# Cos-MLP in three steps an output, weight preparation on an agenda, gate logits from float16 blocks

## The chip, the cores and the metric

One core of a Trainium2 chip runs the whole program. The metric is device time in microseconds, the median of several executions. One further execution was recorded by the hardware profiler; what is said of single instructions comes from that one. Engines carry the names of the profile: PE is TensorE (PEld its weight loads), DVE is VectorE, ACT is ScalarE, POOL is GpSimd, and SP is the queue from which every DMA of this kernel is issued.

## The reference

Three layers follow each other on 2304 tokens of width 512 (4 batches of 576 positions, 8 heads of 64).

```
x = attention(q, k, v, f)                   # causal, with a decay from the running sum of log f
h = x @ w_in;  x = (h * cos(h)) @ w_out     # 512 -> 2048 -> 512; w_in and w_out are float64
logits = x @ w_gate                         # 8 experts
P = exp(logits - max);  8 times: rows to 1, columns to N / 8
out = sum over e of P[:, e] * (relu(x @ w1[e]) @ w2[e])     # 512 -> 1024 -> 512
```

The middle layer is called the Cos-MLP here.

## The kernel before, in words

**Numbers.** A large matmul is made of float16 products. Each operand is scaled by a power of two and split into a high and a low half; three products (high·high, high·low, low·high) give one result. The scale comes from a sum of squares a partition (ScalarE, `Square` with an accumulated output), whose maximum over all partitions everyone needs. `share` (L117) reduces on VectorE, stores the maxima to a small DRAM tensor and at once issues the DMA that reads them back to every partition; `set_scale` (L124) reduces what came back and makes the scale with six small operations on VectorE.

**The queues.** The order of the work is written out by hand (`tc.manual_schedule`): each engine runs its instructions in the order in which the program issues them, and an instruction that waits holds all that are behind it on its engine. SP's DMAs are in order in the same way. Side work (weights, surveys, splits) is written as Python generators; each `next` issues one more piece of them between the pieces of the main work.

**Attention** runs up to about 273 us. Between its steps the generators prepare the first two pairs of Cos-MLP weights (`prepare_pair`, L195) and split the first group of tokens.

**Cos-MLP** (L1227 to L1275). Three groups of 768 tokens, four blocks `b` of hidden units with two pairs of tiles each: 24 items `(b, g, s)`. An item computes four outputs `o` of 128 hidden units by 384 tokens. TensorE gets the first layer of the item (4 × 12 matmuls, L270), then the second layer of the item two before (4 × 12 matmuls, L921). Four PSUM banks hold the first layer's outputs. For every output, all within one turn of the loop: ScalarE takes the whole turns of the phase (L298), VectorE the rest (L299), ScalarE the Sin (L303), VectorE the product (L307, after which the bank is free); one turn later ScalarE casts the high half (L312) and POOL, or VectorE in the last block, subtracts the low half (L314). `leave2` adds a second-layer result to `acc` (ScalarE in block 0, L935; VectorE later, L937).

In between, `later` (L1183) prepares a pair of weight tiles for each three items or so. Four jobs of one 512 KB load each turn float64 bits into float32: POOL L177, VectorE L178, L180, L182 and L185, ScalarE L186. Then come one share of two columns into `room`, the scale, ScalarE's scaling and cast (L212, L214) and POOL's low halves (L218). `load_job` issues the load after next. `split_group` (L236) scales a token group and splits it on ScalarE and POOL, and `find_group` finds its scale. `survey_first` reads expert 0's weights in 16 chunks to find their scale.

At the end the scales of groups 0 and 1 for the experts are found (`look_x`, `share_x`, `set_x`), and the gate logits of these groups are taken as float32 matmuls of `acc` and `w_gate` (`logits`, L939). `expert_prep` makes the first expert's weights and the seven blocks of group 0's input.

**Experts** (from L1593). Sixteen blocks (expert, half) of three token groups each; a group's turn is two first layers (L1370) and one second layer (L1491). `hook` is called 28 times a group, 84 times a block, and issues what `put_at` planned for that slot: weights of the next block, a survey of the next expert's weights (`plan_survey`, L1568), its scale, and in the first two blocks the other groups' inputs, the logits of group 2 and the Sinkhorn steps.

Of the kernel before, what the change touches and what calls it, by code (L numbers as in the profile page):

```python
# [23 lines left out]
def kernel(  # L24
# [13 lines left out]
    nc = tc.nc  # L38
# [39 lines left out]
    sel = const.tile([16, 8], F32, name="sel")  # L78
# [18 lines left out]
    most = keep.tile([P, 2], F32, name="most")  # L97
    sc_w = [keep.tile([P, 2], F32, name=f"scw{x}") for x in range(NW)]
    bk_w = [keep.tile([P, 2], F32, name=f"bkw{x}") for x in range(NW)]
# [5 lines left out]
    xsum = [keep.tile([P, KD], F32, name=f"xsum{x}") for x in range(2 * NG)]  # L105
    sc_x = [keep.tile([P, 1], F32, name=f"scx{x}") for x in range(2 * NG)]
    bk_x = [keep.tile([P, 1], F32, name=f"bkx{x}") for x in range(2 * NG)]
# [16 lines left out]
    def set_scale(room_, k, scale, back):  # L124
        nc.vector.tensor_reduce(back, room_.rearrange("q (p x) -> q x p", x=k), axis=AX.X, op=ALU.max)
# [19 lines left out]
    def share_x(y):  # L145
        share(xsum[y], 1, f"xmost{y}", xroom_of[y])

    def set_x(y):
        set_scale(xroom_of[y], 1, sc_x[y], bk_x[y])


# [18 lines left out]
    def run_job(n):  # L170
# [6 lines left out]
        nc.gpsimd.tensor_tensor(guard, topf, topf, ALU.mult)  # L177
        nc.vector.tensor_scalar(xi, top, 3, 0x3FFFFFFF, ALU.logical_shift_left, ALU.bitwise_and)  # L178
        yield
        nc.vector.scalar_tensor_tensor(xi, top, -0x40000000, xi, ALU.bitwise_and, ALU.bitwise_or)  # L180
        yield
        nc.vector.scalar_tensor_tensor(xi, low, 29, xi, ALU.logical_shift_right, ALU.bitwise_or)  # L182
        load_job(n + 2)
        yield
        nc.vector.scalar_tensor_tensor(x, guard, TINY * TINY, x, ALU.is_ge, ALU.mult)  # L185
        nc.scalar.activation(guard, x, AF.Square, accum_out=wsum[:, y // 2, y % 2 : y % 2 + 1])  # L186
        yield
# [7 lines left out]
    def prepare_pair(u, early):  # L195
        for y in range(4):
            yield from run_job(4 * u + y)
        share(wsum, 2, f"wmost{u}", room)
        yield
        yield  # L200
        yield
        set_scale(room, 2, sc_w[u], bk_w[u])
        nc.vector.tensor_tensor(both[:, u : u + 1], bk_w[u][:, 0:1], bk_w[u][:, 1:2], ALU.mult)
        yield
        todo = [(tmps[y], d(u, 0), d(u, 1), sc_w[u][:, y : y + 1]) for y, d in enumerate((in_of, out_of))]
        for t, hi, lo, sc in todo:
            if early:
                nc.gpsimd.tensor_scalar(t, t, sc, 0.0, ALU.mult, ALU.add)
                yield
                nc.gpsimd.tensor_scalar(hi, t, 1.0, 0.0, ALU.mult, ALU.add)  # L210
            else:
                nc.scalar.activation(t, t, AF.Copy, scale=sc)  # L212
                yield
                nc.scalar.copy(hi, t)  # L214
            yield
        for t, hi, lo, sc in todo:
            for c in range(0, 2 * DM, 2 * P):
                nc.gpsimd.tensor_tensor(lo[:, c : c + 2 * P], t[:, c : c + 2 * P], hi[:, c : c + 2 * P], ALU.subtract)  # L218
                if c % DM:
                    yield  # L220
# [3 lines left out]
    def find_group(g, junk):  # L224
        for x in range(KD):
            look_x(g, g, junk, x)
            if x % 2:
                yield
        share_x(g)
        yield  # L230
        yield
        yield
# [3 lines left out]
    def split_group(g):  # L236
        X = X_of[g]
        for x in range(KD):
            a = acc[:, x, group(g)]
            nc.scalar.activation(a, a, AF.Copy, scale=sc_x[g])  # L240
            yield
            for t in range(2):
                a = acc[:, x, cols(g, t)]
                hi, lo = (X[PLACE[x // 2, t]][:, y, x % 2, :] for y in range(2))
                nc.scalar.copy(hi, a)
# [4 lines left out]
    xroom_of = [xroom] * (NG + 1) + [None, None]  # L250
# [44 lines left out]
    def phase(b, g, s, o, ps):  # L295
        t = draw("t")
        sc = turnv[:, 2 * b + s, g : g + 1]
        nc.scalar.activation(t.bitcast(I32), ps, AF.Identity, bias=quarter, scale=sc)  # L298
        nc.vector.scalar_tensor_tensor(t, ps, sc, t.bitcast(I32), ALU.mult, ALU.subtract)  # L299
        return t  # L300
# [9 lines left out]
    def split_h(b, g, s, o, G):  # L310
        H = draw(f"t{o % 2}")
        nc.scalar.copy(H[:, 0, :], G)  # L312
        eng = nc.vector if b == NW // 2 - 1 else nc.gpsimd
        eng.tensor_tensor(H[:, 1, :], G, H[:, 0, :], ALU.subtract)  # L314
        H_of[b, g, s, o] = H

    with tc.manual_schedule():

        with ExitStack() as actx:
# [141 lines left out]
            nc.gpsimd.tensor_tensor(sel, ident[0:16, 0:8], ident[0:16, 8:16], ALU.add)  # L461
# [321 lines left out]
            pieces = chain(prepare_pair(0, True), prepare_pair(1, True))  # L783
# [37 lines left out]
            for x in range(-9, NSTEP + PS):  # L821
# [7 lines left out]
                if x == 8 * PS + 6:  # L829
                    splitting = chain(find_group(0, junk), split_group(0))  # L830
                if x == 12 * PS + 6:
                    splitting = chain(splitting, find_group(1, junk))
                if x >= 4 and x % 2 == 0:
# [809 lines left out]
```

## Time and profile before

| | |
|---|---|
| median of 3 runs | 2123.81 us (2122.56 to 2125.36) |
| the profiled execution | 2126.4 us, its span 2124.6 us |
| TensorE | busy 1979.3 us, 93% of the span |
| VectorE | 1471.5 us, 69% |
| ScalarE | 1269.9 us, 60% |
| GpSimd | 1110.6 us, 52% |
| mean granted TensorE clock | 0.975 |

The span runs from the first to the last instruction. A busy share is a mean over stages of different kinds. In a row of groups, the time behind the bar is the sum of the group's instructions, then the mean of one, then how long the engine stood idle just before them, and what ended that idle time.

### The profile page before, as it was taken

What the parts mean: (1) busy time and instruction counts of PE and PEld (TensorE: products, weight loads), DVE (VectorE), ACT (ScalarE), POOL (GpSimd) and SP (SyncE); (2) the same over time, 40 slices, a digit from 0 to 9 for tenths busy, and PEclk for the clock granted to TensorE, in tenths of its full rate; (3) what the DMA queues carried; (4) which work ended last, traced back from release to release, by engine and by line L of the source; (5) the groups of instructions that cost most, each with busy time, mean ns of one, the idle gap of its engine ahead of it and who ended that gap; (6) DMA issues with size and microseconds to landing.
All of it is one profiled execution on the core that took longest, in us unless ns stands there. A gap on an engine that the chain in (4) does not pass through costs nothing.

```text
span 2124.6 us, 41207 instructions
## 1 busy us (share of the span) xinstructions
PE 1979.3 (93%) x15493; PEld 1446.6 (68%) x15493; DVE 1471.5 (69%) x3385; ACT 1269.9 (60%) x2698; POOL 1110.6 (52%) x1439
## 2 busy tenths in 40 slices
PE   7897859788999998999999999999999999999998
PEld 6786735454556666677777777677777767777776
DVE  8878745566655345778777777777777777777776
ACT  6787756564556457656556656556656655655543
POOL 7676634333434357655465555554555645555531
PEclk9999989999999899999999999999999999999999
DMA  5444311232010013313303203313223222321122
GB/s 133 101 97 103 51 32 52 67 97 48 21 33 11 24 63 122 115 46 127 95 31 126 102 21 132 100 35 120 63 85 107 75 81 69 107 85 45 49 83 60
DMA packets 145128, 160.19 MB, mean 75 GB/s; under 512 B 68128, under 2 KB 96928, under 8 KB 144928
## 3 DMA queue, kind: packets, MB, share of 16 engines
q1 hardware_dynamic: 144928, 157.55, 25.5%
q8 instruction: 122, 2.00, 0.4%
q14 instruction: 78, 0.64, 0.1%
HBM read 142.20 MB, written 10.39 MB: 72 GB/s over the span
## 4 chain that ended last, share of the span: by engine, by line
PE 64%; DVE 7%; DMA 7%; ACT 5%; POOL 2%; issue 2%; SPq 0%; DVEq 0%; POOLq 0%; ACTq 0%
PE y L1491 17%; PE y L1370 15%; PE bq L1491 13%; PE bq L1370 11%; PE a L921 4%; PE ph L270 3%; DMA xs<-emost 2%; DMA room<-wmost 1%; DMA emost<-most 1%; DVE tm L185 1%; DMA wmost<-most 1%; DVE tm L180 1%; DVE t L307 1%; DMA xmost<-most 1%; DVE t L299 1%
## 5 line engine op out<-in xcount | busy, mean ns | idle before, releaser
L1491 PEld LDWEIGHTS <-h 128*128 128x128 f16 x6048 | 595.3, 98 | 77.6 <-DVE h L1396 0.5
L1370 PEld LDWEIGHTS <-wi 128*128 128x128 f16 x4032 | 395.5, 98 | 289.3 <-issue 37.4
L1370 PE MATMUL y<-xc,wi 128*128 128x384 f16 x2304 | 431.5, 327 | 27.6 <-DVE bq L1390 18.0
L1405 POOL TENSOR_TENSOR h<-t,h 128x384 f16<-128x384 f32 x192 | 175.3, 913 | 480.5 <-ACT h L1404 460.3
L1491 PE MATMUL y<-wb,h 128*128 128x256 f16 x3456 | 415.0, 275 | 0.0
L1370 PE MATMUL bq<-xc,wi 128*128 128x384 f16 x1728 | 329.7, 327 | 0.8 <-ACT t L1386 0.8
L1386 ACT ACTIVATE t<-y 128x384 f32<-128x384 f32 x192 | 94.2, 491 | 377.9 <-PE y L1370 377.9
L1491 PE MATMUL bq<-wb,h 128*128 128x256 f16 x2592 | 307.1, 273 | 0.2 <-DVE h L1396 0.2
L270 PE MATMUL ph<-xc,wi 128*128 128x384 f16 x1152 | 211.4, 344 | 54.8 <-DVE t L307 54.8
L1472 DVE SCALAR_TENSOR_TENSOR acc<-y,gate,acc 128x256 f32<-128x256 f32 x504 | 212.5, 477 | 50.8 <-PE y L1491 50.2
L270 PEld LDWEIGHTS <-wi 128*128 128x128 f16 x1152 | 117.8, 102 | 144.2 <-issue 78.3
L921 PE MATMUL a<-h,wo 128*128 128x384 f16 x1152 | 197.4, 332 | 11.6 <-DVE acc L937 11.2
L1472 DVE SCALAR_TENSOR_TENSOR acc<-bq,gate,acc 128x256 f32<-128x256 f32 x378 | 159.6, 478 | 40.0 <-PE bq L1491 39.6
L921 PEld LDWEIGHTS <-wo 128*128 128x128 f16 x1152 | 114.4, 99 | 90.5 <-issue 18.4
L1396 DVE TENSOR_TENSOR h<-bq,h 128x384 f16<-128x384 f32 x288 | 157.3, 550 | 8.5 <-ACT h L1393 6.5
L314 POOL TENSOR_TENSOR h<-t,h 128x384 f16<-128x384 f32 x72 | 66.7, 927 | 183.2 <-ACT h L312 164.1
L1390 DVE SCALAR_TENSOR_TENSOR bq<-bq,t 128x384 f32<-128x384 f32 x192 | 107.6, 561 | 70.5 <-PE bq L1370 65.6
L1393 ACT CAST h<-bq 128x384 f16<-128x384 f32 x288 | 136.0, 486 | 12.5 <-DVE bq L1447 12.3
L1390 DVE SCALAR_TENSOR_TENSOR bq<-y,t 128x384 f32<-128x384 f32 x96 | 54.3, 565 | 119.9 <-PE y L1370 102.9
L1399 POOL TENSOR_TENSOR h<-st,h 128x384 f16<-128x384 f32 x96 | 88.0, 916 | 83.8 <-ACT h L1393 82.8
L1403 ACT ACTIVATE t<-bq 128x384 f32<-128x384 f32 x192 | 94.7, 493 | 37.5 <-DVE bq L1390 35.6
L299 DVE SCALAR_TENSOR_TENSOR t<-ph,turnv,t 128x384 f32<-128x384 f32 x96 | 58.8, 613 | 64.2 <-ACT t L298 64.1
(250 smaller groups left out, 3360.4 us busy)
## 6 DMA issues: line engine op xcount, KB each, us to landing
xc<-xd SPq DMA_DIRECT2D x105, 384.0 KB
xs<-in_moe_w_dram SPq DMA_DIRECT2D x112, 256.0 KB
sg<-in_moe_w_dram SPq DMA_DIRECT2D x44, 512.0 KB
wo<-in_moe_w_dram SPq DMA_DIRECT2D x20, 512.0 KB
sg<-in_moe_w_in_dram SPq DMA_DIRECT2D x16, 512.0 KB
sg<-in_moe_w_out_dram SPq DMA_DIRECT2D x16, 512.0 KB
xd<-xc SPq DMA_DIRECT2D x14, 384.0 KB
q<-q SPq DMA_DIRECT2D x30, 160.0 KB
```

Of the source, the lines that this page charges most:

```text
L270: nc.tensor.matmul(ps[:, 0:HN], w[ws][:, (2 * kk + f) * P : (2 * kk + f + 1) * P], X_of[g][PLACE[kk // 2, t]][:, xs, kk % 2, :], start=n == 0,
L921: nc.tensor.matmul(ps[:, 0:HN], out_of(2 * b + x, ws)[:, f * DM + d * P : f * DM + (d + 1) * P], H[:, hs, :], start=n == 0, stop=n == 11,)
L1370: nc.tensor.matmul(ps[:, 0:HN], w[:, ws, a, k, :], X[b][:, xs, k, :], start=fresh and n == 0, stop=n == 5, skip_group_check=not fresh,)
L1386: nc.scalar.activation(c, cut(ps), AF.Copy, scale=RAISE)
L1390: nc.vector.scalar_tensor_tensor(cut(c), cut(ps), RAISE, other, ALU.mult, ALU.add)
L1393: nc.scalar.copy(HT[m][c][:, 0, :], src)
L1396: nc.vector.tensor_tensor(HT[m][c][:, 1, :], src, HT[m][c][:, 0, :], ALU.subtract)
L1399: nc.gpsimd.tensor_tensor(HT[m][c][:, 1, :], src, HT[m][c][:, 0, :], ALU.subtract)
L1403: nc.scalar.activation(r, cut(ps), AF.Relu)
L1405: nc.gpsimd.tensor_tensor(HT[m][c][:, 1, :], r, HT[m][c][:, 0, :], ALU.subtract)
L1472: nc.vector.scalar_tensor_tensor(a, v, gate[:, tt, e : e + 1], a, ALU.mult, ALU.add)
L1491: nc.tensor.matmul(ps[:, at_ * HD : (at_ + 1) * HD], HT[m][a][:, s1, c * P : (c + 1) * P], W2T[side][m][:, s2, b, :], start=fresh and m == ...
```

## The change

It touches the Cos-MLP, the scales and the first two expert blocks.

- **Outputs in steps.** `phase` becomes `whole` and `rest`, `split_h` becomes `high_h` and `low_h`. A new `step` issues, in this order: whole turns of output o, product of o−2, Sin of o−1, rest of o, low half of o−3, a piece of weight work, high half of o−2. Three empty steps follow the last output. The second layer is issued in the step of the item's second output, and one `leave2` in each step. In item (0, 0) the low halves go to VectorE.
- **Agenda.** `plan_pair` writes each operation of a pair into a numbered step. A pair's jobs are 5 steps apart (4 in the attention), the second pair starts 30 (21) steps after the first; share, fetch and set lie 6 (2) steps apart, and each column has its own share. Two agenda steps an output are issued in items 0 and 1, four in items 2 to 5, three later; what is left is issued when a block of items ends.
- **Scales.** `share` no longer issues the fetch; `fetch` is a call of its own. All shares have one column. `find_x` finds two of the groups' scales by a transpose and a matmul on TensorE in place of the DMAs.
- **Logits.** `w_gate` is scaled and split into float16 halves early (`split_gate`). The logits of all three groups are taken in the experts' first block, in slots 16, 40 and 54, from the float16 blocks of the experts' input: 60 matmuls a group with 16 columns. VectorE puts the two halves together in three operations. The Sinkhorn steps start in slot 58.
- **Split of groups.** Group 1's high halves are copied on POOL; group 2's split begins at the end of item 2.
- **Surveys.** Experts 0 and 1 are both surveyed within the Cos-MLP. The later ones start with expert 2 in the third block; looks lie at slots 8, 10 and then every third from 38, each chunk's load one slot after the look that frees its buffer; share, fetch and set in slots −5, 1 and 11 around the block's end.

```diff
-    def share(cols, k, name, room_):
-        m = most[:, 0:k]
-        d = sdram.tile([P, k], F32, name=name)
+    def share(cols, name):
+        m = mosts[n % len(mosts)]
+        shared[name] = sdram.tile([P, 1], F32, name=name)
         nc.vector.tensor_reduce(m, cols, axis=AX.X, op=ALU.max)
-        nc.sync.dma_start(d, m)
-        nc.sync.dma_start(room_, d.rearrange("p x -> (p x)").partition_broadcast(P))
+        nc.sync.dma_start(shared[name], m)
+
+    def fetch(name, room_):
+        nc.sync.dma_start(room_, shared[name].rearrange("p x -> (p x)").partition_broadcast(P))
...
+    def find_x(y, bank):
+        gm, gr = mosts[y % 3], mosts[3 + y % 3]
+        nc.vector.tensor_reduce(gm, xsum[y], axis=AX.X, op=ALU.max)
+        yield
+        ps = bank()
+        nc.tensor.transpose(ps[0:1, 0:P], gm, ident)
+        nc.vector.tensor_reduce(gr[0:1, 0:1], ps[0:1, 0:P], axis=AX.X, op=ALU.max)
+        yield
+        ps = bank()
+        nc.tensor.matmul(ps[:, 0:1], ones[0:1, :], gr[0:1, 0:1], start=True, stop=True)
+        nc.vector.tensor_copy(bk_x[y], ps[:, 0:1])
+        make_scale(sc_x[y], bk_x[y])
+        yield
...
+    def plan_pair(agenda, u, base, gap, lag, early):
+        for y in range(4):
+            plan_job(4 * u + y, lambda n, fn, y=y: at_(gap * y + n, fn), gap)
+        for y, d in enumerate((in_of, out_of)):
+            n = gap * (2 * y + 1) + 7
+            at_(n, lambda y=y: share(wsum[:, y, :], f"wmost{u}{y}"))
+            at_(n + lag, lambda y=y, row=row: fetch(f"wmost{u}{y}", row))
+            n += 2 * lag
+            at_(n, lambda row=row, sc=sc, bk=bk: set_scale(row, sc, bk))
...
+        def logits(g, X, bank):
+            for x in range(TT):
+                t, c = divmod(x, TT // 2)
+                todo = [(B11, 0), (B21, 2)] if t == 0 else [(T1, 0), (B11, 0), (B22, 2)]
+                for blk_, k0 in todo:
+                    for k in range(2):
+                        for y in range(2):
+                            nc.tensor.matmul(
+                                ps[:, x * 2 * NE : (x + 1) * 2 * NE],
+                                X[blk_][:, y, k, c * P : (c + 1) * P],
+                                wg[:, k0 + k].rearrange("p y e -> p (y e)"),
...
+        def step(new):
+            if new:
+                key, ps = new
+                t = whole(*key, ps)
+            m = None
+            if waved:
+                mk, mps, mt = waved.pop(0)
+                m = (*mk, product_of(*mk, mps, mt))
+            if shaped:
+                z = shaped.pop(0)
+                wave(z[2])
+                waved.append(z)
+            if new:
+                rest(*key, ps, t)
+                shaped.append((key, ps, t))
+            if high_:
+                low_h(*high_.pop(0))
+            next(pieces, None)
+            if m:
+                high_h(*m)
+                high_.append(m)
...
             for o in range(4):
+                step(((b, g, x, o), outs[o]))
+                if n >= 2 and o == 1:
+                    pb, pg, _ = items[n - 2]
+                    rest_of = layer2(pb, pg, x)
+                if waiting:
+                    leave2(*waiting.pop(0))
+                waiting += rest_of
+                next(pieces, None)
+                next(looking, None)
+                next(splitting, None)
...
-            first, step = (53, 2) if blk == 0 else (2, 5)
             for n in range(NSEEN):
-                put_at(base + first + step * n, lambda n=n: (look(e, n), load_chunk(e, n + 2)))
+                when = (8, 10)[n] if n < 2 else 32 + 3 * n
+                put_at(base + when, lambda n=n: look(e, n))
+                put_at(base + (when + 1 if n >= 2 else 16 + 2 * n), lambda n=n: load_chunk(e, n + 2))
```

## Rows read from the trace of the kernel before

**Rows 1.** Stretches (start:end, length, busy us of each engine, granted clock, DMA, GB/s).

```profile
391.60:547.40 155.80, 130.63 (x770) 75.98 (x769) 98.29 (x191) 82.66 (x171) 56.84 (x64) 0.98 0.26 72
547.40:679.70 132.30, 127.29 (x770) 75.86 (x769) 78.49 (x152) 73.05 (x125) 56.82 (x74) 0.97 0.10 26
...
751.30:837.10 85.80, 77.32 (x529) 55.42 (x528) 43.05 (x107) 59.76 (x138) 62.48 (x73) 0.92 0.17 58
```

**Rows 2.** Timeline of TensorE (start, length, line, output, count, idle time before).

```profile
299.21 7.00 PE L270 MATMUL ph<-xc,wi 128*128 128x384 f16 x24 [5.34 <-DVE t L307]
...
547.39 7.96 PE L270 MATMUL ph<-xc,wi 128*128 128x384 f16 x48
555.19 7.96 PE L921 MATMUL a<-h,wo 128*128 128x384 f16 x48
...
695.29 7.99 PE L944 MATMUL ph<-wgr,acc 128*128 128x8 f32 x48
703.13 6.43 PE L270 MATMUL ph<-xc,wi 128*128 128x384 f16 x24
...
734.92 6.79 PE L944 MATMUL ph<-wgr,acc 128*128 128x8 f32 x48
741.55 9.90 PE L921 MATMUL a<-h,wo 128*128 128x384 f16 x48
751.30 1.14 PE L1370 MATMUL y<-xc,wi 128*128 128x384 f16 x6
```

**Rows 3.** Groups of instructions, 264 to 752 us (count, busy us, mean ns, idle before).

```profile
L270 PE MATMUL ph<-xc,wi 128*128 128x384 f16 x1152 | 211.4, 344 | 54.8 <-DVE t L307 54.8
...
L298 ACT ACTIVATE t<-ph,quarter,turnv 128x384 int32<-128x384 f32 x96 | 63.3, 659 | 57.7 <-PE ph L270 32.2 <-DVE turnv L289 21.7 <-DVE down L291 3.8
L307 DVE SCALAR_TENSOR_TENSOR t<-ph,lift,t 128x384 f32<-128x384 f32 x96 | 58.9, 613 | 60.7 <-ACT t L303 56.7 <-POOL h L314 2.7 <-POOL xc L246 0.9
...
L303 ACT ACTIVATE t<-t,shift 128x384 f32<-128x384 f32 x96 | 58.6, 610 | 15.0 <-DVE t L299 14.5
...
L240 ACT ACTIVATE acc<-acc,scx 128x768 f32<-128x768 f32 x8 | 7.5, 932 | 0.0
L245 ACT CAST xc<-acc 128x384 f16<-128x384 f32 x16 | 7.4, 509 | 0.3
...
L125 DVE TENSOR_REDUCE bkw<-room 128x2 f32<-128x256 f32 x6 | 2.5, 420 | 28.9 <-DMA room<-wmost 28.9
...
L125 DVE TENSOR_REDUCE bkx<-xc 128x1 f32<-128x128 f32 x3 | 0.9, 286 | 25.8 <-DMA xc<-xmost 25.8
```

**Rows 4.** Timeline of SP's queue: a share and its fetch, twice.

```profile
300.38 0.33 SPq L121 DMA_DIRECT2D xmost<-most  x1
308.15 0.33 SPq L122 DMA_DIRECT2D xc<-xmost  x1
...
321.66 0.34 SPq L121 DMA_DIRECT2D wmost<-most  x1
324.72 0.34 SPq L122 DMA_DIRECT2D room<-wmost  x1
```

**Rows 5.** One tile's instructions, sg, 264 to 600 us (ns least, median, most).

```profile
L180 DVE SCALAR_TENSOR_TENSOR tm<-sg,tm x24: 674/997/1428, 279.0 to 580.7; 128x512 int32<-128x512 int32 x24
```

**Rows 6.** Timeline of TensorE at the end of the attention.

```profile
255.27 0.79 PE L711 MATMUL pv<-v,A 128*128 128x65 bf16 x20
```

**Rows 7.** Who TensorE waited for among the experts (total us, times, longest).

```profile
PE y L1370 <- DVE bq L1390: 18.0, 8, 3.0
PE y L1370 <- ACT t L1386: 9.6, 7, 3.1
```

**Rows 8.** Timeline of TensorE, expert 2's scale being set.

```profile
1044.98 1.21 PE L1370 MATMUL y<-xc,wi 128*128 128x384 f16 x6 [2.82 <-DVE bq L1390]
```

**Rows 9.** Timeline of ScalarE, a survey's chunk in the experts' first block.

```profile
829.55 0.63 ACT L887 ACTIVATE xs<-xs 128x512 f32<-128x512 f32 x1 [5.82 <-DMA xs<-in_moe_w_dram]
```

**Rows 10.** Timeline of VectorE, the same scale as in rows 8.

```profile
1040.94 0.42 DVE L125 TENSOR_REDUCE bkwe<-xs 128x2 f32<-128x256 f32 x1 [1.23 <-DMA xs<-emost]
```

More of the change, by code (lines that the diff above doesn't have):

```diff
@@ L222, with run, find_group @@
+    def run(agenda):
+        for n in range(max(agenda) + 1):
+            for fn in agenda.get(n, []):
+                fn()
+            yield
     PLACE = {(0, 0): B11, (0, 1): T4, (1, 0): B21, (1, 1): B22}
-    def find_group(g, junk):
+    def find_group(g, junk, lag):
         for x in range(KD):
@@ L241, in split_group @@
             yield
+        for x in range(KD):
             for t in range(2):
@@ L1147, in expert_prep @@
                     load_raw(n + 2)
-            while now[0] < len(items) - 1:
+            while not scaled:
                 yield
@@ L1181 @@
         now = [0]
-        def later():
-            for u in range(2, NW):
-                gen = prepare_pair(u, False)
-                for _ in range(20):
-                    next(gen)
-                    yield
-                while now[0] < 6 * (u // 2 - 1) + 2 and u >= NSLOT:
-                    yield
-                yield from gen
-            while now[0] < 6 * (NW // 2 - 1):
-                yield
-            yield from expert_prep()
         def survey_first():
+            yield from split_gate()
@@ L1197, in survey_first @@
             while now[0] < 6:
                 yield
-            load_chunk(0, 0)
-            load_chunk(0, 1)
-            yield
-            yield from survey(0)
-            share_w(0)
-            yield
-            yield
-            set_w(0)
-            yield
-        pieces = later()
+            for e in range(2):
+                yield from survey(e)
+                yield
+                share_w(e)
+                for _ in range(3):
+                    yield
+                fetch_w(e)
+                for _ in range(4):
+                    yield
+                set_w(e)
+                yield
@@ new lines @@
+            if n and n % 6 == 0:
+                drain(pieces)
+                if b < last_b:
+                    agenda = {}
+                    for y in range(2):
+                        plan_pair(agenda, 2 * b + 2 + y, 30 * y, 5, 6, False)
+                    pieces = run(agenda)
+                else:
+                    drain(looking)
+                    pieces = expert_prep()
+            if n == 0:
+                factors(b, g, x)
+            outs = []
+            for o in range(4):
+                outs.append(ahead[o] if n == 0 and o in ahead else layer1_part(b, g, x, o, bank1(o)))
@@ L1260 @@
+            if (n + 1) % 6 == 0 and n + 1 < len(items):
+                drain(pieces)
+                factors(*items[n + 1])
+        for y in range(3):
+            step(None)
+            if y == 1:
+                rest_of = layer2(last_b, NG - 1, 0)
+            if waiting:
+                leave2(*waiting.pop(0))
+        waiting += rest_of
         for x in range(KD):
             look_x(NG + 1, 1, junk_c, x)
-        share_x(NG + 1)
-        kept_banks[1] = logits(1, bank_h)
-        for _ in range(4):
+        scale1 = find_x(NG + 1, bank_h)
@@ L1272 @@
             leave2(*y)
-        for _ in chain(pieces, looking, splitting):
-            pass
+        drain(pieces)
         assert not step_of
```

345 lines of the change are left out of this document (192 added, 153 removed).

## The prediction

> **What bounds the kernel now.** I read the stretches first, then TensorE's timeline, then who holds whom in the Cos-MLP, then the queue of SP. TensorE is the busiest engine, but unevenly. From 547.4 to 679.7 us its two blocks of 48 matmuls follow each other at 555.19 − 547.39 = 7.80 us a block, without a gap [rows 2], and it is busy for 127.3 of 132.3 us. The same loop from 391.6 to 547.4 keeps it busy for 130.6 of 155.8 us, though VectorE is then busy for only 98.3 of them and ScalarE for 82.7 [rows 1]. So no engine is full there: the order of the queues loses the time.
>
> Where: first-layer matmuls wait 54.8 us for the product on VectorE, which frees their PSUM bank. That product itself waits 56.7 us for ScalarE's Sin, because whole turns, Sin and product of one output stand behind each other. And VectorE, whose queue is in order, stands 28.9 us in front of `room` and 25.8 us in front of the x scales, for DMAs that carry maxima to DRAM and back [rows 3].
>
> Work of the matmuls alone, from the first layer of item 2 (299.21) to the experts' first matmul (751.30): 22 first-layer and 24 second-layer blocks are left, 46 × 7.80 = 358.8 us. The stretch takes 452.1, so 93.3 us are not such blocks. Of them the two float32 logit blocks take 7.84 + 6.63 = 14.5 us [rows 2]; the other 78.8 are waits and the slow clock after them (granted 0.98 and 0.97 in the two stretches above, 0.92 in the experts' first block [rows 1]).
>
> **The change part by part.**
>
> *Attention and items 0 and 1.* The same weight work comes a little earlier there, with the fetch two steps behind the share. I take 0; the ends are −4 and +4, half of a mean x-scale wait (25.8 / 3 = 8.6 us [rows 3]) gone or new. Items 0 and 1 have no second layer, so the queues pace them, as now. What is new: group 1's high halves are copied on POOL and the last of them comes at the end of item 1, just where the first layer of item 2 needs it: +2 us, up to +6, nothing gained.
>
> *Three steps an output.* ScalarE's work for one output stays 659 + 610 + 506 ns as shown (casts like those of L245 stand for the last, 509 ns), VectorE's twice 613 [rows 3]. But in a step whole turns of output o, Sin of o−1 and product of o−2 are issued, so none of them waits for the other's result of the same step. Per item of two blocks TensorE needs 15.6 us; VectorE's 98.3 us over the eight items of the busier stretch are 12.3, ScalarE's 10.3 [rows 1]. Both fit, so TensorE should set the pace from item 3 on. The bank of an output is held longer. The fourth bank is the tight one: item n+1 writes it 5.85 us after its start, and the product that frees it stands behind whole turns of the next output (ready at 1.95 + 0.66), its rest (0.61), an accumulation (0.61) and three agenda steps. Of VectorE's 98.3 us in eight items, 8 × 12 × 0.613 = 58.8 are such operations; the rest, 39.5, is weight work: 4.9 us an item, 0.41 an agenda step at 12 an item. So the product ends near 2.61 + 1.22 + 1.23 + 0.61 = 5.7 us, just in time, but the work is lumpy. I charge 0.5 us for each of 16 items with weight work: 8 us; the ends are 0 and 46 (rival 2).
>
> *Scales put apart.* Share, fetch and set are now six agenda steps from each other, 12 steps an item, so 15.6 / 12 × 6 = 7.8 us. Shares are now of 4 bytes a partition throughout. In the trace such a share takes 308.15 − 300.38 = 7.8 us until SP can issue its fetch; one of 8 bytes takes 324.72 − 321.66 = 3.1 [rows 4]. The new lag is thus just used up, and where four agenda steps go to an output (items 2 to 5) SP stands some 2 us. VectorE's set comes another 7.8 us later, and the 54.7 us of waits go nearly whole. Behind a standing fetch on SP wait weight loads and survey chunks; I charge nothing here, and price it as rival 3.
>
> *Items 3 and 4.* By the rows of ScalarE in [rows 3], group 2's scaling and casts stay on ScalarE, all within item 3: 4 × 0.93 + 8 × 0.46 + 4 × 1.78 for the outputs are 14.5 us, and four evacuations and weight work bring it to about 18 against 15.6, and item 4 cannot start before the last low half on POOL. I charge 6 us for it (0 to 10), and 2 for item 2's uneven start.
>
> *The end of the Cos-MLP.* The two float32 logit blocks leave, 14.5 us. The waits for the two groups' x scales go (8.6 us each in the mean): group 0's fetch comes an output ahead of its set, with the store two outputs before that. Group 1's scale is found by a transpose and a matmul, 0.7 us of TensorE instead of a DMA. Late next is the experts' first input, a chain of casts on ScalarE and subtractions on POOL; it starts with the last item's second output and has three second-layer blocks (23.4 us) to hide behind. I charge 2 us, up to 8.
>
> Sum of the stretch: 358.8 + 0.7 + 8 + 6 + 2 + 2 = 377.5 instead of 452.1, −74.6 us.
>
> *Experts.* Three logit blocks of 60 float16 matmuls replace the third float32 one. The nearest row has 20 matmuls with new weights and 65 columns in 0.79 us [rows 6], so 180 cost at most 7.1 us against 6.6: +0.5, −5 to +6.
> A rule speaks for more. The Trainium skill, "TensorE: Matmul & The Clock Gate", Back-to-back issue gap, gives about 81 ns for each pair of weight load and matmul with 128 columns in a stream. By that rule 180 would take 14.6 us and the total would be 7 us longer; the row has half that price a pair, so I stay with the row.
> The survey of expert 1 leaves block 0. There ScalarE stands 5.82 us for a chunk that lies behind stores on SP [rows 9], and TensorE waits for ScalarE 9.6 us in all [rows 7]. I take 5.5 of it off and leave the rest to the group work, and half of what the clock of 0.92 loses there (0.08 × 85.8 = 6.9 us): 3.5. VectorE's set of an expert's scale costs TensorE 2.82 us where I looked, 18.0 over eight stalls [rows 7, 8]; 1.23 of the hold is the DMA [rows 10]. That goes, but the set becomes two chains of seven small operations instead of one, so VectorE is held longer by work. I take 7 of the 18 off (0 to 15). Together 0.5 − 5.5 − 3.5 − 7 = −15.5.
>
> **Sum.** 2 − 74.6 − 15.5 = −88.1 on the profiled execution's 2126.4 us is 2038.3. That execution lies 2.6 us above the median of the runs, so I predict 2036 us.
>
> **The rivals.**
> 1. *Nothing is left over.* None of the new stalls comes (18 us in the stretch, 2 before), and the experts gain 11 us more, within their ends: 2036 − 20 − 11 = 2005. For it: the stretch from 547 us on already runs without gaps. Against: it has little weight work.
> 2. *VectorE still paces the items with weight work.* Where the three agenda steps hold three operations of a job at 1.0 us, the middle of L180 [rows 5], instead of 1.23 in all, the product ends at 7.4 us and the fourth bank is late by 1.6; with all three at L180's longest, 1.43, by 2.9: 16 × 1.6 − 8 = 18 to 16 × 2.9 − 8 = 38 us more, 2054 to 2074. For it: VectorE at 12.3 of 15.6 us is the fullest queue beside TensorE. Against: a late output can be made good in the next.
> The Trainium skill, "GPSIMD Engine Reference", Specifications, says that POOL shares its SBUF interfaces with VectorE, with contention where VectorE reads two SBUF inputs. The spread of L180, which has two, agrees; as copies move to POOL, the rule speaks for this rival.
> 3. *Slower: SP's queue.* A load is issued five agenda steps (6.5 us) ahead of its job, behind whatever SP stands at. If fetches hold each of the 24 loads up, VectorE waits in front of each job, for 7.8 us at most, 187 in all. From 88 / 24 = 3.7 us a load on the change is a loss; in the middle, 5.7 us, it ends at 2036 + 137 = 2173. For it: the 4-byte share is that slow. Against: only a third of the loads has a fetch before it, and the lag is as long as the share.
> 4. *It does not do what it says*: the order of one queue (ScalarE's Sin behind the next output's whole turns) keeps the waits as they are, and only the logits and the experts gain: 2123.8 − 14.5 − 15.5 = 2094. Against it: that Sin is issued a step after its input.
>
> **How the numbers follow.** Forecast 0.53, with 2018 to 2054 as its own range; rival 1 0.12; rival 2 0.24; rival 3 0.06, of it 0.01 within the bound; rival 4 0.05. The range is 2008 to 2080: it leaves out half of rival 1, a little of rival 2, and rivals 3 and 4. What a measurement of this kernel can tell from no change is about 0.2%, 4 us. Faster by more: 0.53 + 0.12 + 0.24 + 0.05 = 0.94; within it 0.01; slower 0.05.
>
> **What would show it.** Right: item starts 15.6 to 16.1 us apart from item 4 to 23; no VectorE wait for `room` or the x scales above 2 us; first-layer waits for the product under 15 us in all; the experts' first matmul near 679 us; float16 logits at 40 ns a matmul or less; no wait for a chunk in block 0. Wrong: items still near 18 to 19.5 us apart (rival 2), weight jobs that wait for their loads (rival 3), or an experts' stretch that is as long as now.

## The result, and the profile after

The kernel after takes 2072.06 us (median of four executions, 2069.03 to 2075.0), the kernel before 2123.76 on the same chip: a ratio of 0.9756 with a 95% interval of 0.9738 to 0.9774, 51.7 us less. The forecast was 2036, its range 2008 to 2080. The profiled executions differ by 4 us more, with spans of 2124.6 and 2068.5 us, as the one before is slower than its median and the one after faster. By stretches of these spans:

| stretch | before | forecast of the change | after | change |
|---|---|---|---|---|
| start to the first Cos-MLP matmul | 264.74 | 0 | 254.28 | −10.5 |
| from there to item 2 (299.21, now 285.80) | 34.5 | +2 | 31.5 | −3.0 |
| item 2 to the experts' first matmul (751.30, now 697.10) | 452.1 | −74.6 | 411.3 | −40.8 |
| experts to the end | 1373.3 | −15.5 | 1371.4 | −1.9 |

So more came from the attention than was forecast, and 34 us of the Cos-MLP's and 14 of the experts' gain are missing. The −10.5 is one trace against one: the traces of four other kernels below with the same attention start the Cos-MLP at 255.4 to 258.0 us, which makes the gain 7 to 10.5 us.

Three stretches of the trace after, answering to [rows 1]: items 6 to 13, items 14 to 21, and the first 85.8 us of the experts. The columns are those of [rows 1].

```profile
367.90:510.60 142.70, 129.25 (x771) 75.91 (x769) 92.14 (x197) 81.69 (x175) 53.33 (x58) 0.98 0.41 76
510.60:647.20 136.60, 127.25 (x769) 75.60 (x768) 83.23 (x196) 80.96 (x156) 58.69 (x76) 0.99 0.25 56
697.10:782.90 85.80, 68.28 (x635) 49.95 (x634) 52.71 (x96) 52.64 (x119) 58.85 (x68) 0.90 0.19 67
```

Eight items take 142.7 and 136.6 us where 8 × 15.6 = 124.8 would do. The second eight even take 4.3 us longer than before (132.3). The experts' first block runs at a granted clock of 0.90, no better than the 0.92 of before.

The groups of the Cos-MLP after (254 to 698 us), answering to [rows 3]:

```profile
L307 PE MATMUL ph<-xc,wi 128*128 128x384 f16 x1152 | 207.7, 340 | 44.2 <-DVE t L346 34.3 <-POOL xc L284 4.7 <-POOL xc L281 4.4
...
L346 DVE SCALAR_TENSOR_TENSOR t<-ph,lift,t 128x384 f32<-128x384 f32 x96 | 58.4, 609 | 0.0
...
L950 ACT ACTIVATE seen<-seen 128x512 f32<-128x512 f32 x32 | 20.0, 626 | 17.1 <-DMA seen<-in_moe_w_dram 17.1
...
L132 DVE TENSOR_REDUCE bkw<-room 128x1 f32<-128x128 f32 x12 | 3.4, 279 | 18.9 <-DMA room<-wmost 18.9
...
L132 DVE TENSOR_REDUCE bkx<-xc 128x1 f32<-128x128 f32 x3 | 0.8, 283 | 1.8 <-DMA xc<-xmost 1.8
```

The product no longer waits for Sin (56.7 us before, 0.0 now), the waits for maxima fell from 54.7 to 20.7, but TensorE still waits 44.2 us in front of the first layer. Of the 18.9 us for `room`, 17.6 are two waits, at the ends of the second and the third block of six items. ScalarE waits 17.1 us for chunks of the surveys (`seen`, L950). VectorE at the two ends, and TensorE a little later:

```profile
467.49 0.28 DVE L132 TENSOR_REDUCE bkw<-room 128x1 f32<-128x128 f32 x1 [9.37 <-DMA room<-wmost]
...
576.59 0.29 DVE L132 TENSOR_REDUCE bkw<-room 128x1 f32<-128x128 f32 x1 [8.22 <-DMA room<-wmost]
```

```profile
482.25 4.00 PE L307 MATMUL ph<-xc,wi 128*128 128x384 f16 x12 [5.12 <-DVE t L346]
...
587.18 3.04 PE L307 MATMUL ph<-xc,wi 128*128 128x384 f16 x9 [4.33 <-DVE t L346]
```

SP's queue ahead of the first of them shows where the time goes. The pair's last share stands directly in front of the two shares of the survey:

```profile
446.22 0.33 SPq L126 DMA_DIRECT2D wmost<-most  x1
446.60 0.90 SPq L126 DMA_DIRECT2D emost<-most  x2
454.42 0.32 SPq L129 DMA_DIRECT2D room<-wmost  x1
454.84 9.02 SPq L129 DMA_DIRECT2D seen<-emost  x2
463.91 0.42 SPq L954 DMA_DIRECT2D seen<-in_moe_w_dram  x1
```

Each share has 4 bytes a partition. SP reaches the first fetch 8.2 us behind its share, stands almost 9 us more in front of the last of the two others, and VectorE gets `room` 13.1 us after its fetch was issued. What holds that fetch itself so long the trace does not show.

In the experts one instruction makes the difference. VectorE, then GpSimd, then TensorE:

```profile
747.33 0.56 DVE L1573 TENSOR_TENSOR bq<-y,st 128x384 f32<-128x384 f32 x1
747.80 14.37 DVE L1031 TENSOR_TENSOR bkg<-bkx,wgbk 128x1 f32<-128x1 f32 x1
762.27 0.27 DVE L1032 TENSOR_SCALAR gate<-bq,bkg 128x48 f32<-128x48 f32 x1
```

```profile
760.02 1.45 POOL L1132 TENSOR_TENSOR tm<-sg 128x256 f32<-128x256 f32 x2
761.38 0.77 POOL L1132 TENSOR_TENSOR tm<-tm,sg 128x256 f32<-128x256 f32 x1
762.23 0.72 POOL L1132 TENSOR_TENSOR tm<-sg,tm 128x256 f32<-128x256 f32 x1
```

```profile
762.90 2.74 PE L1617 MATMUL bq<-wb,h 128*128 128x256 f16 x12 [14.48 <-DVE gate L1033]
```

A product of one number a partition, of two SBUF tensors, takes 14.37 us; its two sisters take 0.15 and 0.26. From before 747 us GpSimd's instructions follow each other without a gap (each starts before the end of the one ahead of it), until the one that ends at 761.38 + 0.77 = 762.15. The next starts at 762.23, and VectorE's instruction ends at 762.17.

### The profile page after: what moved, and what is told of

It is laid out like the page before. It is cut to its first block, busy times and chain, and to the rows that moved or that the text cites. A ratio compares the mean times of both kernels' runs of the same rounds, so it can differ in the third digit from the quotient of the medians.

```text
span 2068.5 us, 41510 instructions
## 1 busy us (share of the span) xinstructions
PE 1945.6 (94%) x15535; PEld 1421.6 (69%) x15535; DVE 1492.4 (72%) x3537; ACT 1259.6 (61%) x2692; POOL 1113.9 (54%) x1441
## 4 chain that ended last, share of the span: by engine, by line
PE 73%; DVE 10%; ACT 7%; DMA 6%; issue 2%; POOL 1%; SPq 0%; DVEq 0%; ACTq 0%; POOLq 0%
PE y L1617 17%; PE y L1496 17%; PE bq L1617 13%; PE bq L1496 13%; PE a L989 5%; PE ph L307 4%; DMA seen<-in_moe_w_dram 2%; DMA room<-wmost 1%; DMA wmost<-most 1%; PE pv L752 1%; PE pst L702 1%; DMA qr<-in_q_dram 1%; ACT t L334 1%; DVE bkg L1031 1%; DVE A L722 1%
## 5 line engine op out<-in xcount | busy, mean ns | idle before, releaser
L1617 PEld LDWEIGHTS <-h 128*128 128x128 f16 x6048 | 592.3, 98 | 104.5 <-DVE gate L1033 14.8
L1531 POOL TENSOR_TENSOR h<-t,h 128x384 f16<-128x384 f32 x192 | 175.6, 914 | 452.1 <-ACT h L1530 442.6
L1617 PE MATMUL y<-wb,h 128*128 128x256 f16 x3456 | 409.8, 273 | 0.0
L1617 PE MATMUL bq<-wb,h 128*128 128x256 f16 x2592 | 309.1, 273 | 27.7 <-DVE gate L1033 14.5
L307 PE MATMUL ph<-xc,wi 128*128 128x384 f16 x1152 | 207.7, 340 | 44.2 <-DVE t L346 34.3
L989 PE MATMUL a<-h,wo 128*128 128x384 f16 x1152 | 192.4, 327 | 1.0 <-issue 0.6
L334 ACT ACTIVATE t<-ph,quarter,turnv 128x384 int32<-128x384 f32 x96 | 63.8, 665 | 82.8 <-PE ph L307 69.6
```

Source lines behind the costliest of these rows:

```text
L307: nc.tensor.matmul(ps[:, 0:HN], w[ws][:, (2 * kk + f) * P : (2 * kk + f + 1) * P], X_of[g][PLACE[kk // 2, t]][:, xs, kk % 2, :], start=n == 0,
L989: nc.tensor.matmul(ps[:, 0:HN], out_of(2 * b + x, ws)[:, f * DM + d * P : f * DM + (d + 1) * P], H[:, hs, :], start=n == 0, stop=n == 11,)
L1531: nc.gpsimd.tensor_tensor(HT[m][c][:, 1, :], r, HT[m][c][:, 0, :], ALU.subtract)
L1617: nc.tensor.matmul(ps[:, at_ * HD : (at_ + 1) * HD], HT[m][a][:, s1, c * P : (c + 1) * P], W2T[side][m][:, s2, b, :], start=fresh and m == ...
```

## The experiments

Medians in us. A batch shares one chip and one set of runs of the kernel before, so ratios compare across batches. The time of before was 2122.91 in the first batch, 2119.49 in the second, 2124.18 in the third.

| run | batch | time | ratio, 95% |
|---|---|---|---|
| scalar form of `bkg` | 1 | 2051.41 | 0.9671, 0.9646 to 0.9697 |
| two-column shares | 1 | 2041.44 | 0.9623, 0.9599 to 0.9647 |
| group 1 split on ScalarE | 1 | 2067.99 | 0.9734, 0.9690 to 0.9777 |
| attention's fetches chained | 1 | 2077.87 | 0.9792, 0.9762 to 0.9821 |
| both (scalar form, two columns) | 2 | 2024.86 | 0.9553, 0.9527 to 0.9579 |
| logits of group 1 later | 2 | 2052.78 | 0.9681, 0.9656 to 0.9706 |
| both, outputs in one step | 2 | 2022.40 | 0.9542, 0.9519 to 0.9564 |
| both, splits earlier | 2 | 2024.38 | 0.9552, 0.9529 to 0.9576 |
| both, steps one apart | 3 | 2077.03 | 0.9781, 0.9760 to 0.9802 |
| both, experts' scales apart | 3 | 2015.98 | 0.9493, 0.9472 to 0.9513 |
| the last, outputs in one step | 3 | 2011.97 | 0.9477, 0.9454 to 0.9501 |
| after, outputs in one step | 3 | 2073.51 | 0.9764, 0.9744 to 0.9784 |

**The slow VectorE instruction.**

```diff
-            nc.vector.tensor_tensor(bkg, bk_x[NG + g], wgbk, ALU.mult)
+            nc.vector.tensor_scalar(bkg, bk_x[NG + g], wgbk, None, ALU.mult)
```

> One edit: the gate logits' factor bkg = bk_x * wgbk (128x1) is formed by a tensor_scalar with wgbk as its per-partition scalar instead of a tensor_tensor of two SBUF tensors. Nothing else differs. Theory A (the two-input form cannot go on while GpSimd runs its combine subtractions back to back, 740 to 762): the call that took 14.37 us at 747.80 takes under 0.4 us, TensorE's wait of 14.48 us at 762.90 goes, and with the half-clock stretch behind it the whole falls by 14 to 18 us, to 2054 to 2058. Theory B (VectorE stood there for something the call needs, the scale of group 0 or of the gate weights, or for the logits' bank): the same 14 us stay in the same place in another form, 2070 to 2074.

2051.41 us, and the experts' stretch took 698.29 to 2052.5, 1354.2 us instead of 1371.4. The call at the same place, beside the same unbroken run on GpSimd:

```profile
748.99 0.20 DVE L1031 TENSOR_SCALAR bkg<-bkx,wgbk 128x1 f32<-128x1 f32 x1
```

The block's first 85.8 us now have a clock of 1.00. Theory A holds: the gain is 21 us by the medians and 18 by the ratios, a little more than expected. The second run keeps the form and moves the place:

```diff
-        for g, x in enumerate((16, 40, 54)):
+        for g, x in enumerate((16, 52, 54)):
```

> The kernel after with one edit: group 1's gate logits and their leaving stand 12 slots later in the experts' first block (slots 52 and 54 instead of 40 and 42), behind the end of GpSimd's run of subtractions; bkg keeps its two-input tensor_tensor. Theory A (that form starves only while GpSimd's instructions follow one another without a gap): all three calls take under 1 us, and the whole is 2051 to 2058, as with the scalar form. Theory B (the call is slow for its operands or as the first of its kind behind some other work): 14 us again at its new place, 2068 to 2075.

2052.78 us, the gain of the other run. The expectation was wrong on the duration: the slot came sooner than reckoned, 10 us later than before and still inside the run. VectorE and GpSimd there:

```profile
758.00 4.62 DVE L1031 TENSOR_TENSOR bkg<-bkx,wgbk 128x1 f32<-128x1 f32 x1
```

```profile
761.88 0.72 POOL L1132 TENSOR_TENSOR tm<-tm,sg 128x256 f32<-128x256 f32 x1
762.68 0.72 POOL L1132 TENSOR_TENSOR tm<-sg,tm 128x256 f32<-128x256 f32 x1
```

It began 10.2 us later and took 9.8 us less. Its end hardly moved (762.17, now 762.62): it is again at GpSimd's first break (762.60 to 762.68), and TensorE no longer waits for it. Changing the form at the same place removes the loss, so late data do not explain it; changing the place with the same form removes it too, so the operands do not either. No run puts a gap into GpSimd's work, so that its gapless run is the cause rests on the ends that coincide.

**The shares.**

```diff
-    mosts = [keep.tile([P, 1], F32, name=f"most{x}") for x in range(6)]
+    mosts = [keep.tile([P, 2], F32, name=f"most{x}") for x in range(6)]
...
-        shared[name] = sdram.tile([P, 1], F32, name=name)
-        nc.vector.tensor_reduce(m, cols, axis=AX.X, op=ALU.max)
+        shared[name] = sdram.tile([P, 2], F32, name=name)
+        nc.vector.tensor_reduce(m[:, 0:1], cols, axis=AX.X, op=ALU.max)
```

The second column is zero; the fetched rows are 256 values wide, and the two of a pair of weights now land in the same `room` one after the other.

> One edit: each share of a maximum through DRAM writes two float32 per partition (the maximum and a zero) instead of one, and the fetch brings back 256 instead of 128 values. Theory A (the 4-byte share itself is what is slow: in the kernel before six one-column shares held SyncE 44.9 us in all, 7.5 each, and sixteen two-column ones 45.4 us, 2.8 each): the shares' landing falls from 7.5 to about 3 us, VectorE's waits of 9.37 and 8.22 us for the second weight scale at 467.49 and 576.59 go, items 12 and 18 take 16 to 18 us instead of 25 and 22, some of ScalarE's 17.1 us of waits for survey chunks go, and the whole falls by 12 to 20 us, to 2052 to 2060. Theory B (a share is slow by what lies ahead of it in the queues, the survey chunks and raw weights): its landing stays at 7 us or more and the time at 2068 to 2076.

2041.44 us, 31 us less than after by the medians and 28 by the ratios, more than expected. SP's waits for shares, in the whole kernel after and then in this one (total, times, longest):

```profile
SPq L129 <- DMA wmost<-most: 75.1, 14, 8.5
...
SPq L129 <- DMA emost<-most: 61.1, 9, 8.2
...
SPq L129 <- DMA xmost<-most: 14.0, 2, 7.1
```

```profile
SPq L129 <- DMA emost<-most: 21.6, 10, 3.2
...
SPq L129 <- DMA wmost<-most: 14.2, 6, 3.4
...
SPq L129 <- DMA xmost<-most: 5.4, 2, 2.8
```

No wait for a share is over 3.4 us, VectorE no longer waits for `room` at all, and ScalarE's 17.1 us of waits for chunks are gone:

```profile
L307 PE MATMUL ph<-xc,wi 128*128 128x384 f16 x1152 | 200.4, 332 | 29.3 <-DVE t L346 17.7 <-POOL xc L284 5.0 <-POOL xc L281 4.4
...
L132 DVE TENSOR_REDUCE bkw<-room 128x1 f32<-128x256 f32 x12 | 4.9, 407 | 0.0
```

The first Cos-MLP matmul comes at 244.52 instead of 254.28, the experts' at 663.10 instead of 697.10: 9.8 us from the attention (9 to 14 over all traces that have the steps apart), 24.2 from the Cos-MLP. Items 14 to 21 now take 126.4 us. The 14.39-us instruction is still there. Both edits in one kernel:

> The scalar form of bkg and the two-column shares together. Theory A (two separate losses, one in the experts' first block, one on the way of the maxima in attention and Cos-MLP): their gains of 20.7 and 30.6 us add, 2017 to 2024. Theory B (both gave the same slack to one engine, GpSimd or SyncE): the sum falls short by 10 us or more, 2030 to 2041.

2024.86 us: by ratios the two gains add (0.9756 − 0.9671 = 0.0085 and 0.9756 − 0.9623 = 0.0133 make 0.0218; 0.9553 is 0.0203 below 0.9756), so the two losses are separate. TensorE's first layer in this kernel, which the later runs start from:

```profile
L307 PE MATMUL ph<-xc,wi 128*128 128x384 f16 x1152 | 200.3, 332 | 28.8 <-DVE t L346 18.5 <-POOL xc L284 5.1 <-POOL xc L281 3.0
```

**Steps put apart or chained.** In the attention alone, in the kernel after:

```diff
-            at_(n + lag, lambda y=y, row=row: fetch(f"wmost{u}{y}", row))
+            at_(n if early else n + lag, lambda y=y, row=row: fetch(f"wmost{u}{y}", row))
...
         share_x(g)
-        for _ in range(lag):
-            yield
         fetch_x(g)
-        for _ in range(lag):
+        for _ in range(2 * lag):
             yield
```

> One edit, in attention alone: each fetch of a maximum is issued directly behind its share (as the kernel before has it) instead of two steps later; the scale is set at the same step. Theory A (in the kernel before SyncE stood 7.5 to 8.3 us in the share's landing while loads and stores of attention queued behind it, the 2.90 us that TensorE waited for q at 249.90 and the 3.46 us of VectorE at 248.92 among them, and putting the steps apart is why attention ends 10.5 us sooner): the first Cos-MLP matmul goes from 254.3 to 258 to 264, and the whole to 2076 to 2082. Theory B (the gain in attention comes from where the weight work's steps stand on VectorE and GpSimd): 253 to 256 and 2070 to 2074.

2077.87 us, 6 us more than after by the medians and 8 by the ratios, whose intervals overlap. The trace is clearer: the first Cos-MLP matmul stands at 265.33, outside the 254.3 to 258.0 of the five traces with steps apart, and the attention's whole gain is gone. SP's waits in front of fetches in the attention (60 to 262 us) are 42.5 us, as theory A has it:

```profile
SPq L129 <- DMA wmost<-most: 27.4, 4, 7.3
...
SPq L129 <- DMA xmost<-most: 15.1, 2, 7.9
```

In the kernel after the same two make 12.1 us, and another 6.8 us of waits for shares lie in front of loads of the attention (L396).

In the Cos-MLP alone, on the kernel with both edits:

```diff
-            plan_pair(agenda, 2 + y, 30 * y, 5, 6, False)
+            plan_pair(agenda, 2 + y, 30 * y, 5, 1, False)
...
```

> The kernel with the scalar form and the two-column shares (2024.9 us); in Cos-MLP each weight maximum is fetched one step behind its share and its scale set one step behind the fetch, instead of six and six. Theory A (the steps put apart are what took the waits for the maxima off VectorE): each of 12 scales waits 3 to 5 us again, 36 to 60 us of VectorE, and a third to two thirds of it reaches TensorE: 12 to 40 us more, 2037 to 2065. Theory B (with shares of 3 us VectorE has room for these waits): 0 to 8 us more, 2023 to 2033.

2077.03 us, some 50 us more, and more than theory A's 12 to 40; the experts' first matmul comes at 718.16 instead of 662.45. All twelve scales wait again:

```profile
L307 PE MATMUL ph<-xc,wi 128*128 128x384 f16 x1152 | 215.3, 346 | 67.7 <-DVE t L346 57.3 <-POOL xc L281 4.4 <-POOL xc L284 3.6
...
L132 DVE TENSOR_REDUCE bkw<-room 128x1 f32<-128x256 f32 x12 | 5.0, 420 | 70.1 <-DMA room<-wmost 70.1
```

Of 70.1 us that VectorE waits, 57.3 − 18.5 = 38.8 come through to TensorE as waits for the product, and its first-layer matmuls are busy 15.0 us longer at 346 instead of 332 ns each: 53.8 of the 54.7 us that the Cos-MLP grew by.

**The outputs' three steps.** `step` does whole turns, rest, Sin and product of one output, and both float16 parts of the output before it:

```diff
                 t = whole(*key, ps)
...
+                rest(*key, ps, t)
+            if high_:
+                m = high_.pop(0)
+                high_h(*m)
+                low_h(*m)
+            next(pieces, None)
             if new:
...
+                wave(t)
+                high_.append((*key, product_of(*key, ps, t)))
```

> The kernel with both edits (scalar form, two-column shares), and the Cos-MLP's outputs in one step again as the kernel before has them: whole part, rest, Sin and product of an output in the same step, the float16 parts in the next. Theory A (VectorE's 56.7 us of waits for Sin in the kernel before were on the path, and the three steps take them off): 20 to 45 us above the kernel with both edits, items of 17 us and more where nothing else is waited for. Theory B (an output's chain fits its 4 us of TensorE in one step as well, as the items of 16.0 us late in the kernel before say): 0 to 12 us above it.

> The kernel after (4-byte shares, two-input bkg) with the Cos-MLP's outputs in one step. Theory A (three steps let outputs run on over VectorE's waits of 8 to 9 us for late scales and the chunk waits of ScalarE): 6 to 25 us above 2072. Theory B (they carry nothing here either): 2066 to 2077.

2022.40 beside 2024.86, and 2073.51 with a ratio of 0.9764 beside 0.9756: no difference in either surrounding. In the first of the two the product waits for Sin again, 30.6 us in 49 waits, and TensorE's waits for the product are not longer but shorter, 8.0 us instead of 18.5:

```profile
L307 PE MATMUL ph<-xc,wi 128*128 128x384 f16 x1152 | 199.4, 332 | 24.8 <-DVE t L346 8.0 <-POOL xc L281 7.6 <-POOL xc L284 7.4
...
L346 DVE SCALAR_TENSOR_TENSOR t<-ph,lift,t 128x384 f32<-128x384 f32 x96 | 59.0, 615 | 34.5 <-ACT t L342 30.6 <-POOL h L357 3.0
```

The zero is a sum, though. By the item starts of the two traces, items 0 and 1 are 4.1 us shorter in one step, items 2 to 4 are 8.1 us longer, and items 5 to 23 are 3.6 us shorter. TensorE's waits in front of the fourth output in items 3 to 17, in three steps and then in one:

```profile
305.81 2.11 PE L307 MATMUL ph<-xc,wi 128*128 128x384 f16 x12 [1.43 <-DVE t L346]
...
361.94 2.11 PE L307 MATMUL ph<-xc,wi 128*128 128x384 f16 x12 [0.61 <-DVE t L346]
...
411.40 2.11 PE L307 MATMUL ph<-xc,wi 128*128 128x384 f16 x12 [1.86 <-DVE t L346]
...
461.91 2.11 PE L307 MATMUL ph<-xc,wi 128*128 128x384 f16 x12 [3.54 <-DVE t L346]
...
510.51 2.11 PE L307 MATMUL ph<-xc,wi 128*128 128x384 f16 x12 [1.23 <-DVE t L346]
```

```profile
526.13 2.11 PE L307 MATMUL ph<-xc,wi 128*128 128x384 f16 x12 [0.76 <-DVE t L346]
```

**The splits of groups 1 and 2.** `split_group(1, False)` in place of `split_group(1, True)`:

> One edit: the float16 high parts of group 1's inputs to Cos-MLP are copied on ScalarE instead of GpSimd. Theory A (GpSimd, which has eight copies and eight subtractions of the split beside the weights' first pair, is what item 2 waits for): TensorE's wait of 4.43 us in item 2 goes, ScalarE has room for eight copies in items 0 to 2, and the whole falls by 3 to 6 us, to 2066 to 2069. Theory B (items 0 to 3 are held by ScalarE, which then takes over the wait): items 0 to 3 take 0 to 6 us longer, 2072 to 2078.

The times do not settle it. Three executions took 2066.03 to 2070.80, the profiled one 2052.54; in that one the two-input product of group 1 got through in 0.89 us in the middle of GpSimd's run, which hides what the split does. In the traces of four other kernels with that form at that place it took 14.37 to 14.39, so the loss is likely but not certain in an execution. Group 2's product in the same trace did stand, until GpSimd's break (760.22 + 0.76 = 760.98):

```profile
758.24 2.75 DVE L1031 TENSOR_TENSOR bkg<-bkx,wgbk 128x1 f32<-128x1 f32 x1
```

```profile
760.22 0.76 POOL L1132 TENSOR_TENSOR tm<-tm,sg 128x256 f32<-128x256 f32 x1
761.06 0.73 POOL L1132 TENSOR_TENSOR tm<-sg,tm 128x256 f32<-128x256 f32 x1
```

The trace does say where the wait went: in item 2 TensorE still waits 6.6 us ahead of its first layer, as against 6.5 in the kernel after, now 3.8 of it for the product, 1.5 for GpSimd and 1.3 for ScalarE. Earlier instead, on the kernel with both edits, with group 2's scale fetched and set two outputs sooner:

```diff
...
-                if n == 2 and o == 3:
+                if n == 2 and o == 1:
                     splitting = split_group(2, False)
-                if n == 3:
+                if n in (0, 2, 3):
                     next(splitting, None)
```

> The kernel with both edits, and the split of group 1 at two pieces an output from item 0 on, that of group 2 begun at item 2's second output instead of item 3's first (its scale fetched and set two outputs sooner; the gate weights' maxima come back to a room of their own). Theory A (items 2 and 4 wait for these splits' last subtractions on GpSimd, 17 us over 15.6 an item in items 2 to 4): 8 to 14 us below the kernel with both edits. Theory B (ScalarE and GpSimd have no room for it in items 0 to 2, the wait only moves): 3 us below to 5 us above.

2024.38 beside 2024.86: the waits for GpSimd and ScalarE are gone (10.2 us) and those for the product went from 18.5 to 27.7, in items 0 to 4. Theory B: the wait only moved.

**The experts' scales.** On the kernel with both edits:

```diff
...
-            put_at(base + NB + 11, lambda: set_w(e))
-            put_at(base + NB + 13, lambda: undo_gate(e))
+            put_at(base + NB + 11, lambda: set_w(e, (0,)))
+            put_at(base + NB + 20, lambda: set_w(e, (1,)))
+            put_at(base + NB + 22, lambda: undo_gate(e))
```

> The kernel with the scalar form and the two-column shares (2024.9 us); in each expert the second of the two weight scales is set nine slots behind the first (slots 11 and 20) and the gate's column two slots behind that. Theory A (the 2.14 us that TensorE waits once in each of six experts are the row of 17 small VectorE instructions ahead of the float16 low part it needs): six waits of 2.1 us fall under 0.8, 8 to 14 us less, 2011 to 2017. Theory B (VectorE is full there, the second half only moves the wait): 2 us less to 3 us more.

2015.98 us, 9 us less by the medians and 13 by the ratios. TensorE's wait, with both scales in one slot and then apart:

```profile
PE bq L1619 <- DVE h L1524: 12.8, 6, 2.1
```

```profile
PE bq L1621 <- DVE h L1526: 2.0, 6, 0.3
```

> The kernel of e10_set_apart with the Cos-MLP's outputs in one step. Theory A (the three steps carry nothing once no share is late): within 5 us of e10_set_apart on either side. Theory B (they carry something that e7's 2.5 us hid by chance): 8 us or more above it.

2011.97 us, the fastest here: 112 us below the kernel before, and by ratios some 60 below the kernel after. The intervals of the last two overlap, so the three steps again show nothing.

## Why the prediction was right in the whole and wrong in its steps

The time is 36 us above the forecast and outside the forecast's own range, 2018 to 2054. It lies in 2008 to 2080 because that range makes room for rival 2, and rival 2's cause is not what happened: that the range holds the time is luck. Of the signs that were to show it right, two came, the cheap logits and no wait for a chunk in block 0. The item starts, the wait for `room`, the waits for the product (34.3 us instead of 15) and the experts' first matmul (697 instead of 679) did not, and one sign of being wrong came, an experts' stretch nearly as long as before. What holds is the direction, and that putting the scales apart pays.

**Attention, 0 taken, −10.5 measured: wrong.** The step counted the weight work on the computing engines and bounded the gain by half an x-scale wait. It did not count SP: a chained fetch stands there until its share has landed, up to 7.9 us in the chained run, and the attention's own loads and stores stand behind it. That run gives all of the gain back.

**The three steps of an output: wrong in kind.** "The product itself waits 56.7 us for ScalarE's Sin" was read as a cause. Two runs bring 30 us of that wait back and the time does not change, so it was off the path: TensorE did not need the bank yet. The 8 us charged for the fourth bank were sized well: with no share late, TensorE waits 8.7 us in front of the fourth outputs of items 3 to 17, and 0.8 in one step. So the three steps cost about what was charged there, and over the whole Cos-MLP they gain nothing.

**Scales put apart: right in kind, and the largest part of the gain.** One step apart instead of six costs some 50 us, the size of the waits for maxima in [rows 3]. But "the 54.7 us of waits go nearly whole" failed: 20.7 us stayed. The step that failed is the price of the 4-byte share. [Rows 4] show it, and the text says that the lag is just used up, yet it counts one share at a time. At the ends of two blocks three stand in a row, each behind the last. In the stretch from item 2 on this is 24.2 of the 33.8 us between forecast and measurement: with two columns it takes 387.1 us instead of 411.3. Rival 3 had the place (SP) and the cause, but priced it on the weight loads; it was scales and survey chunks that came late.

**Items 2 to 4, 8 us charged: too low.** Item 5 starts at 352.31, so these three take 352.31 − 285.80 = 66.5 us, 19.7 above 46.8; TensorE waits 4.43 us for GpSimd in item 2 and 3.01 in item 4. The step sized the loss by ScalarE's work alone; it names POOL's last low half but gives POOL no time. Neither copying group 1 on ScalarE nor starting the splits earlier removed the wait, it only moved; that there is no room for it on three engines which carry weight work too is likely and not shown. (The step's 0.46 us a cast are 0.51 in [rows 3], 0.4 us in all.)

**Logits: right.** Sixty float16 matmuls take 1.65 us:

```profile
743.16 1.65 PE L1018 MATMUL bq<-wg,xc 128*128 128x16 f16 x60
```

That is 27.5 ns each and 5.0 us for all, within the bound from [rows 6]. The figure that the prediction set against the row, 81 ns in the Trainium skill, "TensorE: Matmul & The Clock Gate", Back-to-back issue gap, is one for 128 columns; with 16 columns the trace has a third of it.

**Experts, −15.5 taken, −1.9 measured: right but for one instruction.** Without it the stretch is 1354.2 us, 19.1 below before; no chunk is waited for in block 0, and the clock there is 1.00. The step did not price `bkg`, three instructions that it never listed. The Trainium skill, "GPSIMD Engine Reference", Specifications, says that GpSimd's SBUF interfaces are shared with VectorE, with contention for VectorE's instructions of two SBUF inputs. The prediction weighed it for L180's spread in the Cos-MLP (rival 2), where no run shows it to decide. The trace agrees with it at `bkg`, and the measured price, 14.4 us for one instruction beside a gapless run, is far above that spread (0.67 to 1.43 us). Seven of the 18 us of set waits were taken off, and 18.0 became 11.2. The sum is right, its parts are not quite: expert 1's set, 2.6 us, left with its survey, and the other six cost 1.9 us each, now ahead of the second layer (L1617) instead of the first.

**Rivals.** Rival 2's time, 2054 to 2074, holds the result, but not its cause: the missing time is mostly VectorE held by two DMA waits and one starved instruction. The lumps of weight work are in the 8.7 us above, which the forecast had charged.

Open: with two columns the experts take 5 us more than after (1376.3 and 1371.4), of which the wider reduction explains 1.6. No run puts back the float32 logits, the surveys' places or the x scales by DMA alone; what they are worth is read from the traces.

## What to carry to other kernels

A wait in the trace that is long in sum (56.7 us for Sin) is worth nothing until a run shows that what waits is needed sooner. Price the queue that carries small transfers as an engine of its own. When a change splits a transfer, price the new size from its own row and count how many stand in a row at the busiest place. Look for VectorE instructions of two SBUF inputs, however small, beside a stretch where GpSimd has no gap, and give them a scalar form.

## What the runs showed of the hardware

A share of 128 partitions to DRAM holds SP, when the fetch is next in its queue, about 7.5 us with 4 bytes a partition and 2.8 with 8. In the kernel before only the x scales (`xmost`) had shares of 4 bytes, and SP's waits there were (total, times, longest):

```profile
SPq L122 <- DMA xmost<-most: 44.9, 6, 8.3
SPq L122 <- DMA wmost<-most: 22.9, 8, 3.8
SPq L122 <- DMA emost<-most: 22.5, 8, 3.5
```

A VectorE instruction of 128x1 with two SBUF inputs stood up to 14.4 us beside back-to-back two-input work of GpSimd and ended at GpSimd's first break, one of 0.08 us, in three traces (14.37, 4.62 and 2.75 us by where it began); in one execution it got through in 0.89 us without such a break, and why is open.
